# Setting PE's additional waits ahead of their group: the room that a place must leave, four times as large

## Chip, core and metric

The kernel runs on one core of one Trainium2 chip. The metric is the device time of one execution in microseconds (us), as the median of several runs; less is better. The core's engines are named as in the profile: PE (TensorE's matrix products), PEld (its weight loads), DVE (VectorE), ACT (ScalarE), POOL (GpSimd) and SP (SyncE, which issues DMAs here). Each engine works through its own queue of instructions in order, and the queues are kept together by semaphores: an instruction that finishes raises a counter, and another waits until the counter has reached a value.

## What is computed

Four residual steps on one sequence of 2048 positions with 512 features, bfloat16: attention, MLP, attention, MLP, with the same weights in both rounds.

```python
def _A_ref(x, wqkv, wo):
    B, S, D = x.shape
    H = 32; Dh = D // H; W = 256
    qkv = (lambda x, *d: x.transpose(*d))((x @ wqkv).reshape(B, S, 3, H, Dh), 2, 0, 3, 1, 4)
    q, k, v = qkv[0], qkv[1], qkv[2]
    scores = jnp.einsum("bhqd,bhkd->bhqk", q, k) * (Dh ** -0.5)
    idx = jnp.arange(S)
    mask = (idx[:, None] - idx[None, :] >= 0) & (idx[:, None] - idx[None, :] < W)
    scores = jnp.where(mask[None, None], scores, -1e9)
    p = _softmax(scores, axis=-1)
    o = jnp.einsum("bhqk,bhkd->bhqd", p, v)
    return (lambda x, *d: x.transpose(*d))(o, 0, 2, 1, 3).reshape(B, S, D) @ wo

def _B_ref(x, w1, b1, w2, b2):
    h = jnp.einsum("bsd,df->bsf", x, w1) + b1
    h = _gelu(h)
    return jnp.einsum("bsf,fd->bsd", h, w2) + b2

x = A_x
x = x + _A_ref(_layernorm(x, axis=-1), A_wqkv, A_wo)
x = x + _B_ref(_layernorm(x, axis=-1), B_w1, B_b1, B_w2, B_b2)
x = x + _A_ref(_layernorm(x, axis=-1), A_wqkv, A_wo)
x = x + _B_ref(_layernorm(x, axis=-1), B_w1, B_b1, B_w2, B_b2)
```

Each position attends to the 256 positions that end with itself, in 32 heads of 16 features. The MLP's inner width is 1792.

## The kernel before

**Tiles.** The sequence is cut into 16 tiles of 128 positions, which two rounds make 32 steps (`tau`), and into blocks `b` of two tiles. X stays in SBUF for the whole kernel. For each tile a layer norm is made on DVE and POOL (L740 to L750) and turned to put features on partitions: by PE against an identity (L768, `ident,xn` in the profile) or by a transpose on DVE and two DMAs (L757 to L764). PE then makes Q, K and V (`xnTA,Wqkv_sb`, `Wqkv_sb,xnTA` and `Wqkv_sb,xv`), which ACT and DVE take out of PSUM (L725, L727, L853). Attention makes scores in visits of 512 columns for four groups of heads (`QT,KT`, L952 to L959); each visit needs four PSUM banks, and two exponentials on ACT (L965) empty them into E. DVE or POOL mask E (L981). PE multiplies E with V (`E,Va`, L1000 to L1020), DVE turns and normalises the result (L1031 to L1041), PE projects it with Wo (`Wo_sb,OT`, L1069), and DVE adds it to X (L793). The MLP is two chains of products (`xnTB,W_sb`, L1098 and L1109, and `W_sb,gT`, L1121), with GELU on ACT and bias on DVE or ACT between them. The profile shows W1 and W2 both as W_sb, and nearly all products stand under line 32, where a helper records them.

**Order.** What runs where is written out by hand. `ORDER` (L425) is the sequence of some 3170 steps, `TURNS` (L594) says which of two engines takes a step that either could do, and `BANKS` (L610) gives the PSUM banks. `_List.run` (L233) goes through `ORDER` and books a start and an end for every step, from durations written beside the steps and a few constants. So the plan's times are a forecast in nanoseconds, computed when the program is made.

**Waits.** `_Sched.op` (L89) turns each step into a piece of its engine's program and works out which counters it must wait for. It sorts these waits by the planned end of the work that they wait on, latest first (L115), and drops each one that another already implies (L116). `self.when` holds the planned time at which a counter's value is visible (L120), and `start` the planned start of a step.

**Groups and slots.** One step of PE is a group of 1 to some 70 products, each a weight load and a product; a product's place in PE's program is called a slot in the code. `_Slots._next` (L25) puts the waits of a slot in front of its product. One wait can ride on the weight load itself; of several waits on one slot the others become instructions of their own in PE's queue, which the profile shows under line 27.

**Where PE's waits go.** `_Sched.spread` (L135) gives the first wait of a group, the latest by the plan, to the group's first product (L143 to L145). Each other wait is tried on slots ahead of the group, from the nearest back (L150), up to 96 of them (`LOOK`). The walk ends at a slot whose group starts, by the plan, too soon after the wait's work is visible, or whose group the wait's work itself depends on (L152). The first slot on the walk that holds no wait yet takes it (L154). If the walk ends without one, the wait stays on the group's own first product, together with the first. The room that a slot must leave is 1200 ns for a wait on a DMA and 150 ns for a wait on an engine.

Of the kernel before, what the change touches and what calls it, by code (L numbers as in the profile page):

```python
# [55 lines left out]
class _Sched:  # L56
# [78 lines left out]
    def spread(self):  # L135

        prog = self.prog["pe"]
        slots = [(k, i) for k, o in enumerate(prog) for i in range(o["n"])]
        first, taken = {}, {}
        for x, (k, i) in enumerate(slots):  # L140
            if i == 0:
                first[k] = x
        for k, o in enumerate(prog):  # L143
            if o["waits"]:
                taken[first[k]] = [o["waits"][0]]  # L145
        for k, o in enumerate(prog):
            for w in o["waits"][1:]:
                to = first[k]
                need = self.snap[w].get("pe", 0)
                for x in range(first[k] - 1, max(-1, first[k] - self.LOOK), -1):  # L150
                    k2, i2 = slots[x]
                    if need > k2 or self.when[w] + (1200.0 if w[0].startswith("dma") else 150.0) > prog[k2]["start"]:  # L152
                        break
                    if x not in taken:  # L154
                        to = x
                        break
                taken.setdefault(to, []).append(w)
        for o in prog:
            o["at"] = {}
        for x, ws in taken.items():  # L160
            k, i = slots[x]
            prog[k]["at"][i] = [(self.cnt_sem[c], v) for c, v in ws]
# [1046 lines left out]
```

## Time and profile before

| what | value |
|---|---|
| runs shown | 438.74, 438.5 and 439.74 us; median 438.74 |
| the profiled execution's own time | 439.42 us |
| its span, first to last instruction | 437.7 us |
| mean granted clock of TensorE | 0.996 |
| moved by DMA | 22.82 MB, mean 52 GB/s |

The profile is of one execution. A row of the groups names a line, an engine, an operation, what it writes and reads, and how often it ran; after the bar stand busy time, mean ns of one, and the idle time ahead of it with what ended it. A row of the timeline has start and duration in us, engine, line, operation and count, and in brackets the engine's idle time ahead of it with the work whose end released it; rows of one kind that follow each other are merged. A row of the waits names who waited for whom, with total us, number of times and the longest. PE's rows are the products with their pipeline, so a product of 0.38 us can have the next one 0.22 us behind it; PEld's rows are the loads, which overlap them; PEldq stands for instructions of the same queue that are neither.

### The profile page before, as it was taken

The numbers are of one execution on the slowest core, as the hardware profiler recorded it, in microseconds if no ns is written. First come the engines' busy times: TensorE is split into PE (matmuls) and PEld (weight loads), VectorE is DVE, ScalarE is ACT, GpSimd is POOL, SyncE is SP. The second block draws the span as 40 slices with busy tenths as digits, with TensorE's granted clock in tenths as the row PEclk, the third lists the DMA queues.
The fourth block names the chain that finished last, engine by engine and source line by source line (L and its number), as shares of the span: only waits on it lengthen the run. The fifth ranks groups of instructions, "written<-read, shape, count | busy, mean of one in ns | idle before, by whom it ended". The sixth has DMA issues, their size and how long they took to land.

```text
span 437.7 us, 18385 instructions
## 1 busy us (share of the span) xinstructions
PE 420.4 (96%) x8280; PEld 252.6 (58%) x8338; DVE 369.4 (84%) x752; ACT 391.7 (89%) x456; POOL 267.6 (61%) x293
## 2 busy tenths in 40 slices
PE   7999999999799999999999999999999999999996
PEld 5757757655554646555555555644566554454673
DVE  6999999999999998999899878898988883784722
ACT  3999999999999999899898999899889998999551
POOL 6788765958665847456489545774656397464030
PEclk9999999999899999999999999999999999999999
DMA  8930000001311031011031013001240003004001
GB/s 258 371 110 4 3 3 2 3 7 35 88 49 29 25 77 51 13 52 43 22 75 51 13 37 99 4 3 36 60 115 3 3 27 97 1 3 124 25 13 48
DMA packets 39899, 22.82 MB, mean 52 GB/s; under 512 B 24588, under 2 KB 39308, under 8 KB 39820
## 3 DMA queue, kind: packets, MB, share of 16 engines
q1 hardware_dynamic: 39404, 21.24, 16.6%
q8 instruction: 65, 1.06, 1.0%
q10 hardware_dynamic: 416, 0.39, 0.3%
q14 instruction: 14, 0.11, 0.1%
HBM read 13.77 MB, written 7.86 MB: 49 GB/s over the span
## 4 chain that ended last, share of the span: by engine, by line
PE 68%; ACT 24%; DVE 4%; issue 1%; DMA 1%; POOL 1%; ACTq 0%
PE ps L32 67%; ACT E L965 15%; ACT gT L1103 4%; ACT gT L1111 2%; ACT L1103 1%; ACT L965 1%; DMA X<-in_A_x_dram 1%; DVE E L981 1%; PE ps L36 1%; DVE stat L740 1%; DVE KT L853 1%; DVE TT L1031 1%; DVE X L793 0%; ACT L1111 0%; POOL E L981 0%
## 5 line engine op out<-in xcount | busy, mean ns | idle before, releaser
L965 ACT ACTIVATE E<-ps 128x1024 bf16<-128x1024 f32 x300 | 283.5, 1049 | 19.5 <-PE ps L32 18.6
L981 POOL TENSOR_TENSOR E<-E,mask 128x512 bf16<-128x512 bf16 (+1 forms) x132 | 142.1, 1091 | 72.5 <-DVE E L981 30.1
L32 PE MATMUL ps<-xnTB,W_sb 128*128 128x512 bf16 (+1 forms) x560 | 116.3, 337 | 0.2
L32 PE MATMUL ps<-W_sb,gT 128*128 128x512 bf16 (+2 forms) x418 | 106.4, 373 | 3.2 <-issue 2.5
L32 PE MATMUL ps<-xnTA,Wqkv_sb 128*128 128x256 bf16 (+1 forms) x544 | 74.5, 267 | 0.9 <-ACT E L965 0.5
L32 PEld LDWEIGHTS ps<-xnTB,W_sb 128*128 128x128 bf16 x560 | 51.7, 98 | 37.5 <-ACT E L965 0.7
L793 DVE TENSOR_TENSOR X<-X,ps 128x512 bf16<-128x512 bf16 x63 | 42.7, 679 | 27.2 <-PE ps L32 26.7
L32 PE MATMUL ps<-QT,KT 32*128 32x64 bf16 (+3 forms) x2392 | 60.7, 218 | 3.8 <-ACT E L965 2.7
L32 PEld LDWEIGHTS ps<-W_sb,gT 128*128 128x128 bf16 x462 | 40.8, 98 | 38.2 <-ACT E L965 0.5
L32 PEld LDWEIGHTS ps<-QT,KT 32*128 32x128 bf16 x2392 | 34.8, 93 | 47.6 <-ACT E L965 32.3
L981 DVE TENSOR_TENSOR E<-E,mask 128x512 bf16<-128x512 bf16 (+1 forms) x124 | 49.7, 422 | 11.3 <-ACT E L965 10.9
L32 PEld LDWEIGHTS ps<-xnTA,Wqkv_sb 128*128 128x128 bf16 x544 | 47.8, 98 | 16.5 <-ACT E L965 1.0
L1075 POOL TENSOR_TENSOR X<-X,b2b 128x512 bf16<-128x512 bf16 x32 | 36.8, 1154 | 27.6 <-DVE E L981 17.1
L744 POOL TENSOR_TENSOR statmv<-statmv,mhalf 128x1 f32<-128x1 f32 x64 | 35.8, 565 | 26.6 <-DVE statmv L742 26.6
L1100 DVE TENSOR_SCALAR gT<-ps,b1T 128x512 bf16<-128x512 f32 (+1 forms) x72 | 45.6, 650 | 3.9 <-PE ps L32 2.6
L32 PE MATMUL ps<-E,Va 64*17 64x64 bf16 (+3 forms) x3904 | 46.4, 230 | 1.9 <-ACT E L965 0.5
L1031 DVE STREAM_TRANSPOSE TT<-ps 128x1024 f32<-128x1024 f32 x32 | 39.8, 1244 | 8.7 <-PE ps L32 8.4
L1111 ACT ACTIVATE gT<-ps,b1T 128x512 bf16<-128x512 f32 (+1 forms) x68 | 36.5, 585 | 11.7 <-PE ps L32 11.6
L32 PEld LDWEIGHTS ps<-E,Va 64*17 64x17 bf16 x3904 | 37.1, 85 | 15.6 <-PE ps L32 3.9
L740 DVE BATCH_NORM_STATS2 stat<-X 128x6 f32<-128x512 bf16 x64 | 42.8, 675 | 2.6 <-DMA X<-in_A_x_dram 2.3
L853 DVE TENSOR_TENSOR KT<-ps,parmask 128x512 bf16<-128x512 f32 (+1 forms) x68 | 40.9, 644 | 2.6 <-PE ps L32 2.4
L1036 POOL TENSOR_TENSOR TM<-TT 128x512 bf16<-128x512 f32 x25 | 27.7, 1106 | 20.7 <-DVE TT L1034 11.2
(57 smaller groups left out, 383.4 us busy)
## 6 DMA issues: line engine op xcount, KB each, us to landing
scr_x<-xs_ SPq DMA_DIRECT2D x44, 128.0 KB, 1.7
W_sb<-in_B_w_dram SPq DMA_DIRECT2D x2, 1792.0 KB, 15.7
xnTB<-scr_x SPq DMA_DIRECT2D x26, 128.0 KB, 2.6
xnTA<-scr_x SPq DMA_DIRECT2D x18, 128.0 KB, 2.5
out_dram<-X SPq DMA_DIRECT2D x15, 128.0 KB, 1.9
Wqkv_sb<-in_A_wqkv_dram SPq DMA_DIRECT2D x4, 256.0 KB, 5.1
X<-in_A_x_dram SPq DMA_DIRECT2D x1, 1024.0 KB, 10.5
Wqkv_sb<-in_A_wqkv_dram SPq DMA_DIRECT2D x1, 512.0 KB, 6.6
```

What stands on the lines that cost most here:

```text
L32: return self.e.matmul(*a, **k)
L740: add("dve", lambda e, B: e.bn_stats(stat6[:, k6, 0:6], X[:, t, :]), 598, reads=["X%d" % t], writes=["st%d" % k6], prio=prio)
L744: add("pool", lambda e, B: e.tensor_tensor(out=statmv[:, m, 1:2], in0=statmv[:, m, 1:2], in1=mhalf[:], op=ALU.pow), 535, reads=["mv%d" % m ...
L793: add("dve", lambda e, B: e.tensor_tensor(out=X[:, t, :], in0=X[:, t, :], in1=ps[:, B[g][0], :], op=ALU.add), d_psum(512), reads=["X%d" % ...
L853: x = e.tensor_tensor(out=dst.rearrange("p (g s) (a k) -> p s g a k", s=2, a=2)[:, s], in0=src.rearrange("p (g s k) -> p s g k", s=2, k=HK ...
L965: add("act", lambda e, B, g_=g_, gi=gi: e.activation(E[:, 2 * gi : 2 * gi + 2, e0 : e0 + 512], ps[:, B[g_][0] : B[g_][0] + 2, :], AF.Exp, ...
L981: op = lambda e, B, Ew=Ew, Mw=Mw: e.tensor_tensor(out=Ew, in0=Ew, in1=Mw, op=ALU.mult)
L1031: add("dve", lambda e, B: e.transpose(TT[:, s].rearrange("p a c q d -> p a (c q d)"), ps[:, B[g][0] : B[g][0] + 2, :].rearrange("p a n -> ...
L1036: mul = lambda e, B: e.tensor_tensor(out=TM[:, sm].rearrange("p c q a d -> p a (c q) d"), in0=TT[:, s, :, :, :, 0:Dh].rearrange("p a c q d ...
L1075: add("pool", lambda e, B: e.tensor_tensor(out=X[:, t, :], in0=X[:, t, :], in1=b2b[:], op=ALU.add), 1110, reads=["X%d" % t, "b2b"], writes ...
L1100: add("dve", lambda e, B, g=g, fc=fc: e.tensor_scalar(out=gT[:, js % NG, fc, 0:M], in0=ps[:, B[g][0], 0:M], scalar1=b1T[:, fc : fc + 1], s ...
L1111: add("act", lambda e, B, g=g, fc=fc: e.activation(gT[:, js % NG, fc, 0:M], ps[:, B[g][0], 0:M], AF.Gelu_apprx_tanh, bias=b1T[:, fc : fc + ...
```

## The change

One number in `spread` is another: a slot ahead of a group takes a wait on an engine only if its group starts, by the plan, at least 600 ns after the waited-for work is visible, where it was 150 ns. The room for waits on DMAs stays 1200 ns. Waits that no longer find a slot stay on their group's own first product. The lists, the plan's times, the set of waits and everything on the other engines are as before.

```diff
@@ -149,7 +149,7 @@
                 need = self.snap[w].get("pe", 0)
                 for x in range(first[k] - 1, max(-1, first[k] - self.LOOK), -1):
                     k2, i2 = slots[x]
-                    if need > k2 or self.when[w] + (1200.0 if w[0].startswith("dma") else 150.0) > prog[k2]["start"]:
+                    if need > k2 or self.when[w] + (1200.0 if w[0].startswith("dma") else 600.0) > prog[k2]["start"]:
                         break
                     if x not in taken:
                         to = x
```

## The prediction

> **What bounds the kernel now.** I read the page's first and fourth parts, then the waits of PE over the whole span, then the same view from 120 us on.
>
> ```profile
> span 437.7 us, 18385 instructions
> PE 420.4 (96%) x8280; PEld 252.6 (58%) x8338; DVE 369.4 (84%) x752; ACT 391.7 (89%) x456; POOL 267.6 (61%) x293
> ...
> PE 68%; ACT 24%; DVE 4%; issue 1%; DMA 1%; POOL 1%; ACTq 0%
> ```
>
> PE is busy for 420.4 of 437.7 us and holds 68% of the chain that ended last. So PE sets the time, and a change of PE's waits can give back at most PE's idle time, 437.7 - 420.4 = 17.3 us, if it gives anything.
>
> ```profile
> PE ps L32 <- ACT E L965: 4.0, 8, 1.4
> PE ps L32 <- issue: 2.9, 18, 0.2
> ...
> PE ps L32 <- DVE X L793: 0.3, 1, 0.3
> PE ps L32 <- DVE KT L853: 0.2, 1, 0.2
> PE ps L32 <- DVE E L981: 0.2, 1, 0.2
> ```
> ```profile
> PE ps L32 <- issue: 2.7, 17, 0.2
> PE ps L32 <- DVE X L793: 0.3, 1, 0.3
> PE ps L32 <- PE ps L32: 0.3, 1, 0.3
> PE ps L32 <- DVE stat L740: 0.2, 1, 0.2
> ```
>
> The columns are total us, times, longest. The first fence is the whole span, the second 120 us to the end. The eight waits on the exponentials (4.0 us) all lie before 120 us. After it the matrix products were idle for another engine twice, 0.3 + 0.2 us, and once for PE's own earlier result, 0.3 us; the other 2.7 us have no releaser. So for three quarters of the kernel there is next to nothing that a better place of a wait could win.
>
> **What the change moves.** I worked the plan's own starts and ends out from the printed lists (the arithmetic of `_List.run`, `op` and `spread`). PE has 1627 groups with 8338 products, as many as the weight loads that the page counts for PEld. 486 groups wait, with 236 waits beyond their first. In the kernel before, 172 of the 236 sit on a product ahead of their group; 64 stay on their group's own first product, beside the first wait. A second wait on one product takes an instruction of its own, at L27:
>
> ```profile
> L27 PEldq EVENT_SEMAPHORE  x61: 51/51/51, 8.9 to 392.4; - x61
> ...
> L27 PEldq EVENT_SEMAPHORE  x37: 51/51/51, 120.0 to 392.4; - x37
> ```
>
> 61 such instructions (37 of them after 120 us) of 51 ns carry the 64 waits; a few carry two. [...]
>
> Of the 172 waits set back, 35 are on DMAs and keep their 1200 ns. Of the other 137, 71 have less than 600 ns of room on the product where they sit: 40 on DVE, 18 on ACT, 11 on POOL, 2 on PE. These 71 fall to their group's own first product. They belong to 71 different groups, none of which has a second wait there now, so each gets one L27 instruction: 61 + 71 = 132 in all. 34 go ahead of scores (QT,KT), 20 ahead of E,Va products, 17 ahead of projections, transposes and the like; 21 lie before 120 us, 50 after. Nothing else of the program changes: order, banks, engines and DMAs stay, and no other queue gets or loses an instruction.
>
> **Part removed: waiting too early.** A wait that sits ahead of its group can hold work that doesn't need it. By the times in the trace, 7 of the 71 were the last thing that the product in front waited for (at 60.7, 88.0, 202.7, 255.9, 326.4, 363.0 and 372.2 us). Two of them:
>
> ```profile
> 59.85 0.59 PEld L32 LDWEIGHTS ps<-W_sb,gT 128*128 128x128 bf16 x4
> 60.70 0.10 PEld L32 LDWEIGHTS ps<-W_sb,gT 128*128 128x128 bf16 x1 [0.26 <-DVE xnTB L725]
> 61.08 0.11 PEld L32 LDWEIGHTS ps<-QT,KT 32*128 32x128 bf16 x6 [0.28 <-ACT E L965]
> ```
> ```profile
> 59.91 1.24 PE L32 MATMUL ps<-W_sb,gT 128*128 128x512 bf16 x5
> ...
> 61.08 0.40 PE L32 MATMUL ps<-QT,KT 32*128 32x128 bf16 x16
> ```
> ```profile
> 202.29 0.21 PEld L32 LDWEIGHTS ps<-Wo_sb,OT 128*128 128x128 bf16 x2
> 202.68 0.10 PEld L32 LDWEIGHTS ps<-Wo_sb,OT 128*128 128x128 bf16 x1 [0.19 <-DVE X L793]
> 203.13 0.15 PEld L32 LDWEIGHTS ps<-QT,KT 32*128 32x128 bf16 x12 [0.35 <-ACT E L965]
> ```
>
> At 60.70 a product of W_sb and gT waits for a copy into xnTB that it doesn't read: that is the wait of the scores behind it. The last of the four loads before it starts at 59.85 + 0.59 - 0.10 = 60.34, so its load came 0.36 us later. But the scores' first load comes 61.08 - 60.34 = 0.74 us after that load, and the matmul row has no idle bracket (59.91 + 1.24 = 61.15, past 61.08). At 202.68 it is 203.13 - 202.40 = 0.73 us. Beside them a place where the set-back wait (on DVE) had long come, and one with an L27 instruction:
>
> ```profile
> 221.78 0.10 PEld L32 LDWEIGHTS ps<-W_sb,gT 128*128 128x128 bf16 x1
> 222.00 0.10 PEld L32 LDWEIGHTS ps<-Wo_sb,OT 128*128 128x128 bf16 x1
> 222.52 0.17 PEld L32 LDWEIGHTS ps<-QT,KT 32*128 32x128 bf16 x10 [0.42 <-ACT E L965]
> ```
> ```profile
> 259.66 0.75 PEld L32 LDWEIGHTS ps<-W_sb,gT 128*128 128x128 bf16 x4
> 260.83 0.12 PEld L32 LDWEIGHTS ps<-QT,KT 32*128 32x128 bf16 x8 [0.42 <-ACT E L965]
> ```
> ```profile
> L27 PEldq EVENT_SEMAPHORE  x1: 51/51/51, 260.6 to 260.6; - x1
> ```
>
> At 222 us no wait came late, and the same two steps are 222.52 - 221.78 = 0.74 us. So the late loads at 60.70 and 202.68 cost nothing: a load may come up to about 0.36 us after the one before it (the products themselves are 0.22 us apart) and the scores still start on time. It is the same at the other five, whose two steps also add up to 0.74 us. **Gain: 7 x 0 = 0 us.** When the loads come earlier, what is late next is what ends the 0.74 us now, the switch from full products to scores. From the other side, had every late load held the products, the gain would be the excess over 0.22 us, 0.14 us at 60.70 and 0.41 us for all seven.
>
> **Part added: 71 instructions of 51 ns.** At 260.6 us an L27 instruction stands between W_sb and QT,KT. The last of the four loads starts at 259.66 + 0.75 - 0.10 = 260.31, and the scores' first load 0.52 us behind it. Without one, at 222 us, it is 222.52 - 222.00 = 0.52 us. The 51 ns lie beside the running product. The cover is there in all 34 moves ahead of scores and in 19 of the 20 ahead of E,Va, since each stands at such a switch (the other one joins two E,Va groups and waits on PE itself); ahead of the other 17 the products in front, mostly 0.11 or 0.22 us apart, must cover it. The moved semaphore itself is there in time: in this trace all 71 came at least 0.29 us before their group's first load. Behind each new instruction the whole rest of PE's queue is held, and the exponentials on ACT wait for the scores:
>
> ```profile
> L965 ACT ACTIVATE E<-ps 128x1024 bf16<-128x1024 f32 x300 | 283.5, 1049 | 19.5 <-PE ps L32 18.6
> ```
>
> So if the cover is gone at a place, ACT gets its scores 51 ns later. There is one place in this trace where an L27 instruction lies in time that the products lost:
>
> ```profile
> L27 PEldq EVENT_SEMAPHORE  x1: 51/51/51, 109.8 to 109.8; - x1
> ...
> 109.88 0.40 PE L32 MATMUL ps<-QT,KT 32*128 32x64 bf16 x16 [0.27 <-ACT E L965]
> ```
>
> One of 61 pays, so 71 new ones pay 71 / 61 x 51 ns = 0.06 us. The ends are 0 and 71 x 51 ns = 3.6 us; I take 0.1 us, the value of the nearest rows, since the 37 of them after 120 us share 0.8 us of idle time that has a releaser at all.
>
> **Sum:** 0 gained, 0.1 us paid. The profiled execution took 439.42 us (span 437.7 and 1.7 us around it), so 439.5 for it; it is 0.7 us above the median of the runs shown. On the median, 438.74 + 0.1 = **438.8 us**.
>
> **Rivals.**
>
> *The new waits stand on PE's path* (slower). The place is the first product of the 71 groups, the price 51 ns each: 3.6 us for all, 442.4 us; half of them 1.8 us, 440.5 us. It decides where PE's queue has less than 51 ns of work in front when the instruction is reached, as at 109.8. For it: PE is 96% busy, and 17 of the moves have no switch to hide in. Against it: the equal 0.52 us, and 37 such instructions with nearly no idle time of the products. It must be over 1.3 us, more than a third of all places, to be seen. Chance 0.12.
>
> *Waiting later frees PE's clock* (faster). After idle stretches the granted clock fell:
>
> ```profile
> 115.29 0.40 PE L32 MATMUL ps<-QT,KT 32*128 32x128 bf16 x16 [1.37 <-ACT E L965]
> ```
> ```profile
> 116.90:120.30 3.40, 3.40 (x92) 2.22 (x74) 2.73 (x5) 3.03 (x4) 2.72 (x5) 0.50 0.25 82
> ```
>
> For 3.4 us PE had half its clock (the last columns: clock 0.50, DMA share, GB/s); what it lost is at most 1.7 us. If the idle time before were shorter or lay otherwise, it would go: 438.7 - 1.7 = 437.0 us. [...] Against it: the idle time there is ended by ACT, and the two moved waits in it (108.9 and 113.5 us) came over 0.8 us early. A second such stretch would be as much slower. Chance 0.08 for the loss going, 0.02 for one more.
>
> *PE's program is fetched at other points* (slower).
>
> ```profile
> q8 instruction: 65, 1.06, 1.0%
> ```
>
> 1.06 MB in 65 packets took 1.0% of 16 engines' 437.7 us, 1.08 us each. 71 more instructions move the points at which PE needs the next packet. No idle time of a packet's length is in the view of waits after 120 us, so fetches are covered now; one exposed would give 439.9, two 440.9 us. Chance 0.03 for two.
>
> *The change does nothing*: if L27 stays at x61, 438.7 us; that falls within the forecast.
>
> **How the numbers follow.** About 0.3%, 1.3 us, is what a measurement of this kernel can tell from no change. Within it: my forecast, 0.75. Slower by more: 0.12 + 0.02 + 0.03 = 0.17. Faster by more: 0.08. The range for 8 in 10 takes in the forecast with the spread of the runs shown (438.5 to 439.74), most of the gain of the clock, down to 437.4, and the events paying at a little over half the places, up to 440.8.
>
> **What would show it.** Right: L27 with x132; no bracket ended by DVE at the W_sb load near 60.7; 0.52 us from the last full load to the scores where the new instructions stand; the products' idle time within 1 us of 17.3. Wrong: idle brackets at first products of the 71 groups, or ACT's 18.6 us of waiting for PE grown by 1 us or more (the first rival); a clock row without the half (the second); idle time of about 1 us without a releaser (the third). A gain without any change of the clock would mean that early waits held PE by a way that the idle brackets don't show, and that my 0 was wrong.

## The result, and the profile after

The changed kernel takes **443.38 us** (median of 5 runs, 443.17 to 444.87), the kernel before 438.74 us (438.5 to 439.74): 4.64 us more, a ratio of 1.0108 with a 95% interval of 1.0094 to 1.0121. That is slower by over 0.3%, and outside the range of 437.4 to 440.8. The profiled execution of the changed kernel took 444.27 us with a span of 442.5 us, 4.8 us more than the span before.

The page's first rows, the instructions at L27 and PE's waits (total us, times, longest) over the whole span:

```profile
span 442.5 us, 18456 instructions
PE 423.0 (96%) x8280; PEld 253.4 (57%) x8338; DVE 370.3 (84%) x752; ACT 392.4 (89%) x456; POOL 267.8 (61%) x293
```
```profile
L27 PEldq EVENT_SEMAPHORE  x132: 51/51/51, 9.4 to 421.9; - x132
```
```profile
PE ps L32 <- issue: 5.1, 21, 1.3
PE ps L32 <- ACT E L965: 3.6, 7, 1.4
...
PE ps L32 <- DVE TT L1031: 0.8, 1, 0.8
```

The change did what it says: 61 + 71 = 132 instructions at L27. PE's idle time grew from 17.3 to 442.5 - 423.0 = 19.5 us, and the row that grew is the one without a releaser, from 2.9 us (longest 0.2) to 5.1 us (longest 1.3). The row `<- DVE TT L1031` (0.8 us) belongs to it: it is the stop at 314.1 us in the table below, where PEld's waits put the same 0.8 us down to issue. The other 2.6 us of the 4.8 stand as busy time on the page; the starts of the loads, further down, show them better. The longest of those 21 waits is here, in PE's products of the changed kernel; below it the same groups in the kernel before:

```profile
385.51 0.74 PE L32 MATMUL ps<-E,Va 64*17 64x64 bf16 x64
386.18 0.40 PE L32 MATMUL ps<-QT,KT 32*128 32x64 bf16 x16
386.51 0.72 PE L32 MATMUL ps<-E,Va 64*17 64x64 bf16 x59
388.55 0.21 PE L32 MATMUL ps<-E,Va 64*17 64x64 bf16 x5 [1.31 <-issue]
```
```profile
382.16 0.74 PE L32 MATMUL ps<-E,Va 64*17 64x64 bf16 x64
382.84 0.40 PE L32 MATMUL ps<-QT,KT 32*128 32x64 bf16 x16
383.17 0.74 PE L32 MATMUL ps<-E,Va 64*17 64x64 bf16 x64
383.84 1.04 PE L32 MATMUL ps<-xnTB,W_sb 128*128 128x512 bf16 x4
```

A group of 64 products stops after 59 of them. No wait stands there: the kernel puts none inside this group. So what was missing was not data but the next instructions.

Counting shows it. PE's program has two instructions for each of its 8338 products (the load and the product itself) and one for each at L27. I numbered them and looked where a load came later than the usual spacing with no wait in front that had just ended. In the changed kernel there are seven such places, and all have a number that leaves 191 to 193 when divided by 256:

| us | late by us | remainder | us since the end of the last packet on q8 |
|---|---|---|---|
| 101.7 | 0.42 | 192 | 1.46 |
| 113.2 | 1.01 | 191 | 1.41 |
| 263.2 | 0.12 | 192 | 1.30 |
| 286.2 | 0.42 | 193 | 1.68 |
| 314.1 | 0.83 | 191 | 1.41 |
| 326.1 | 0.14 | 193 | 1.53 |
| 388.5 | 1.54 | 191 | 1.47 |

They add up to 4.5 us. In the two rows with remainder 193 an instruction ahead of the load was held up first (a product at 285.93 us, with 0.26 us `<-issue`, and an L27 instruction at 325.9 us), 1.4 us after the packet. So at all seven PE went on 1.3 to 1.5 us after a packet had ended. q8 is a queue that brings instructions (`q8 instruction` on the page): 65 packets for PE's 16,808 instructions, one for every 258.6. With 16,977 of them (the late 240 below) and 17,040 (232 at the start) the pages count 66 packets, each time as many as there are numbers that leave 192. Two views of the stretch before the stop at 388.5 us, the windows and the DMA queues:

```profile
385.54:387.24 1.70, 1.70 (x140) 1.35 (x139) 1.34 (x2) 1.01 (x2) 1.70 (x3) 1.00 0.04 10
387.24:388.54 1.30, 0.00 (x0) 0.00 (x0) 0.00 (x0) 1.30 (x2) 1.30 (x2) 1.00 0.00 0
```
```profile
q8 instruction: 1, 0.02, 2.3%
```

Some 140 loads and as many products overlap these 1.7 us (second and third column); 128 of each, 256 instructions, lie between the two points. Then PE issued none for 1.3 us, and a single packet of instructions came within those 3.0 us. In the kernel before, the part that begins in the same groups takes 7.41 us, with two packets:

```profile
382.48:389.89 7.41, 7.36 (x155) 3.86 (x139) 5.41 (x10) 6.69 (x9) 5.65 (x6) 1.00 0.02 4
```
```profile
q8 instruction: 2, 0.03, 2.3%
```

So in these runs the program comes in parts of 256 instructions, by the remainders and by the count of packets. At each of the seven stops the last packet before it, which PE waited for, had begun only after PE crossed the point before (0.4 to 1.3 us after): no more than the next part was on its way. Where two points lie around E,Va products and scores, PE can run through a part in less time than the fetch needs: 1.7 us here, where 3.0 us passed from crossing one point to being able to cross the next. The 71 new instructions move the points along the program, by 1 after the first and by 71 after the last.

Two further items make up the 4.8 us. Some stops of the kernel before are gone, 0.15 to 0.19 us at 24, 98 and 286 us, and 0.58 us of the second stop is regained just behind it, where PE waited for ACT before. That leaves 4.5 - 0.5 - 0.6 = 3.4 us. And half clock lasted longer, 6.8 us where it was 3.4 us, with some 0.9 us lost between 114 and 119 us:

```profile
115.80:122.60 6.80, 5.98 (x193) 4.05 (x194) 5.04 (x9) 5.34 (x6) 5.21 (x7) 0.50 0.30 78
```

The remaining 0.5 us arises before 6 us, at the start-up products, ahead of the first L27 instruction (9.4 us), so it isn't the change's. With 3.4 + 0.9 + 0.5 = 4.8 us nothing is left over for the 51 ns of the new instructions.

### The profile page after: what moved, and what is told of

Its sections match the earlier page's. It is cut to its first block, busy times and chain, and to the rows that moved or that the text cites. A ratio compares the mean times of both kernels' runs of the same rounds, so it can differ in the third digit from the quotient of the medians.

```text
span 442.5 us, 18456 instructions
## 1 busy us (share of the span) xinstructions
PE 423.0 (96%) x8280; PEld 253.4 (57%) x8338; DVE 370.3 (84%) x752; ACT 392.4 (89%) x456; POOL 267.8 (61%) x293
## 4 chain that ended last, share of the span: by engine, by line
PE 63%; ACT 28%; DVE 4%; issue 2%; DMA 1%; POOL 1%; ACTq 0%
PE ps L32 62%; ACT E L965 17%; ACT gT L1103 5%; ACT gT L1111 3%; ACT L965 1%; ACT L1103 1%; DMA X<-in_A_x_dram 1%; DVE KT L853 1%; DVE TT L1031 1%; PE ps L36 1%; DVE E L981 1%; ACT L1111 1%; DVE stat L740 1%; DVE X L793 0%; POOL E L981 0%
## 5 line engine op out<-in xcount | busy, mean ns | idle before, releaser
L965 ACT ACTIVATE E<-ps 128x1024 bf16<-128x1024 f32 x300 | 283.9, 1040 | 22.3 <-PE ps L32 21.3
L32 PE MATMUL ps<-QT,KT 32*128 32x64 bf16 (+3 forms) x2392 | 61.6, 219 | 4.7 <-ACT E L965 2.7
L1031 DVE STREAM_TRANSPOSE TT<-ps 128x1024 f32<-128x1024 f32 x32 | 39.8, 1244 | 10.7 <-PE ps L32 10.4
```

Of the source, the lines that this page charges most:

```text
L32: return self.e.matmul(*a, **k)
L965: add("act", lambda e, B, g_=g_, gi=gi: e.activation(E[:, 2 * gi : 2 * gi + 2, e0 : e0 + 512], ps[:, B[g_][0] : B[g_][0] + 2, :], AF.Exp, ...
L1031: add("dve", lambda e, B: e.transpose(TT[:, s].rearrange("p a c q d -> p a (c q d)"), ps[:, B[g][0] : B[g][0] + 2, :].rearrange("p a n -> ...
```

## The experiments

Three theories: **fetch** (PE stops where it reaches a part of its program that has not come), **price** (each new instruction costs its 51 ns on PE's path), **place** (waits that come later in the order cost time themselves). What the fetch theory expects was worked out from the trace of before: the times of its loads, points every 256 instructions as counted above, and 3.45 us from crossing one to being able to cross the next. The 3.45 us are an estimate of the author's; at the seven stops above it was 3.0 to 4.0 us. Each median below stands beside the kernel before run on the same chip, with the ratio's 95% interval.

**Only the count, at the start.** All waits as before; 71 added instructions between the two start-up groups:

```diff
+        prog[1]["at"].setdefault(0, []).extend([(self.cnt_sem["dve"], 1)] * 143)
```

(L27 has x132 in this run, 61 + 71: one of the 143 waits needs no instruction, and two each share one.)

> The kernel before, all waits where they were, with 71 waits that are long satisfied put between PE's two start-up groups, so that all of PE's later program stands 71 instructions further on. Fetch theory (PE stops where its program crosses into a part of 256 instructions that has not been fetched, and 71 more instructions move these points into dense stretches): from the times of the groups in the trace of before, the points then fall where ten of them are reached too early, about 1 to 2 us each; 447 to 453 us. Price theory (each added instruction costs its 51 ns on PE's path): at the start PE waits for the first tiles anyway, so at most 71 x 51 ns = 3.6 us less that cover, 438.7 to 441. Place theory (waits that come later in the order cost time of their own): no wait was moved, 438.7.

Measured: 458.31 us against 438.58, ratio 1.0444 (1.0415 to 1.0474). So the fetch theory's 447 to 453 us is missed as well. In the profiled execution (457.88 us) PE's loads are 4.92 us later than in the kernel before from 14 us on, at the added instructions themselves, more than was expected, and 18.45 us later at the end. The 13.5 us between arise in a program in which every wait stands where it stood. PE's waits (the longest is the one at the start) and one of the stops:

```profile
PE ps L32 <- issue: 17.1, 29, 4.1
```
```profile
399.99 0.68 PE L32 MATMUL ps<-E,Va 64*17 64x128 bf16 x46
402.15 0.21 PE L32 MATMUL ps<-E,Va 64*17 64x64 bf16 x7 [1.49 <-issue]
```

Thirteen stops of 0.15 to 1.83 us sum to 15.2 us, all at remainders 191 to 193; some of it is regained behind them. The trace of before gave some 14 us for this shift. Price and place had at most 441 us, and nothing for the 13.5 us behind the start: both fail here.

**The same instructions, no wait moved.** Each of the 71 groups gets a satisfied wait instead:

```diff
+        for k, o in enumerate(prog):
+            for w in o["waits"][1:]:
+                for x in range(first[k] - 1, max(-1, first[k] - self.LOOK), -1):
+                    if w in taken.get(x, ()):
+                        if not w[0].startswith("dma") and self.when[w] + 600.0 > prog[slots[x][0]]["start"]:
+                            o["at"].setdefault(0, []).append((self.cnt_sem["dve"], 1))
+                        break
```

> The kernel before, with every wait where it was set back to, and a second, long satisfied wait on the first product of the same 71 groups. PE's program then has the same length and the same instructions at the same places as the changed kernel's, but no wait is moved. Fetch theory: as the changed kernel, 442.5 to 444. Price theory: also as the changed kernel. Place theory: as before, 438.7, since only satisfied waits were added.

Measured: 443.55 us against 438.58, ratio 1.0091 (1.0062 to 1.0119), the changed kernel's median within 0.2 us. The interval, 2.7 to 5.2 us, is wide because one of the four runs, the only one at full clock, took 441.51 us; the other three took 443.48 to 443.63 us at 0.995 or 0.996. The long stop is at the same product:

```profile
385.56 0.72 PE L32 MATMUL ps<-E,Va 64*17 64x64 bf16 x59
387.90 0.21 PE L32 MATMUL ps<-E,Va 64*17 64x64 bf16 x5 [1.61 <-issue]
```

So 71 more instructions at these places give the loss with no wait moved, and moving the 71 waits adds or wins nothing that these runs can tell. The place theory falls.

**The change on a part of the groups.** Once on the groups before 120 us alone, once on the others:

```diff
-(1200.0 if w[0].startswith("dma") else 150.0)
+(1200.0 if w[0].startswith("dma") else 600.0 if k < 418 else 150.0)
```

and with `k >= 418`.

> The change on the groups before 120 us alone: 21 waits fall to their own group. Fetch theory: of the stops of the changed kernel only those near 101 and 112 us come, about 0.4 and 1.0 us, with the slower clock after them; the later points move by 21 only and stay covered: 439.8 to 441. Price theory: 21 x 51 ns = 1.1 us spread over 21 places, 439.8. Place theory: under half of the loss, about 21 / 71 of it, 440.1. The trace tells them apart: two long stops inside groups, or 21 small ones.

> The change on the groups after 120 us alone: 50 waits fall to their own group. Fetch theory: the stops near 101 and 112 us are gone, and as the count starts at 0 at 120 us the later points move by 0 to 50 instead of 21 to 71; by the times of before only the one near 385 us is left, about 0.7 us: 438.7 to 440. Price theory: 50 x 51 ns = 2.6 us, 441.3. Place theory: 50 / 71 of the loss, 442.

Measured: 440.65 us, ratio 1.0033 (1.0018 to 1.0048), for the 21 waits, and 439.75 us, ratio 1.0029 (1.0016 to 1.0043), for the 50, both against 438.58. With 21 waits the stops at 101.8 and 113.4 us are there (0.88 and 1.00 us; the second below), and a third of 0.46 us at 323.7 us that the working had not shown. With 50 they are not; there is 0.84 us at 386.6 us, as expected, and again 0.53 us at 323.7. Both times are in the fetch theory's ranges; price and place had 441.3 and 442 us for the 50.

```profile
112.33 0.37 PE L32 MATMUL ps<-QT,KT 32*128 32x64 bf16 x11 [0.67 <-ACT E L965]
113.39 0.31 PE L32 MATMUL ps<-QT,KT 32*128 32x256 bf16 x5 [0.69 <-issue]
```
```profile
111.94 0.40 PE L32 MATMUL ps<-QT,KT 32*128 32x64 bf16 x16 [0.67 <-ACT E L965]
112.86 1.05 PE L32 MATMUL ps<-xnTA,Wqkv_sb 128*128 128x256 bf16 x8 [0.51 <-ACT E L965]
```

The first fence has the 21 waits, the second the 50: the same scores, with and without a stop inside the group. The 50 cost no more than the 21, which no equal price for each instruction gives, and by the medians both together cost less than the whole change (2.07 + 1.17 = 3.24 of 4.64 us).

**The 51 ns by themselves.** From 395 us on only three fetch points are left. Every one of PE's last 240 groups gets an instruction of its own:

```diff
+        for o in prog[1387:]:
+            at = o["at"].setdefault(0, [])
+            at.extend([(self.cnt_sem["dve"], 1)] * (1 if at else 2))
```

> The kernel before, and a long satisfied wait as an instruction of its own ahead of each of the last 240 groups of PE (from 395 us on). Price theory: 240 x 51 ns = 12 us, or what part of it stands on the path: 444 to 451. Fetch theory: there are three fetch points left in this stretch, and by the times of before all three have room for the shift: 438.7 to 439.7, that is, the 51 ns lie beside the running products.

Measured: 439.32 us against 438.66, ratio 1.0010 (0.9995 to 1.0025). L27 over the whole span:

```profile
L27 PEldq EVENT_SEMAPHORE  x301: 51/51/51, 8.8 to 432.1; - x151
```

240 x 51 ns = 12.2 us are added to PE's queue, and 0.7 us or nothing to the time: at most 1.1 us by the interval's upper end, 5 ns each. Most of these groups (224 of 240) are MLP products, so this holds for them first of all. For the scores the changed kernel itself has the row to see: at 262.7 us an L27 instruction stands ahead of scores, and their load comes 262.94 - (261.54 + 0.98 - 0.10) = 0.52 us after the last full one, as without.

```profile
261.54 0.98 PEld L32 LDWEIGHTS ps<-W_sb,gT 128*128 128x128 bf16 x6
262.94 0.34 PEld L32 LDWEIGHTS ps<-QT,KT 32*128 32x128 bf16 x16 [0.42 <-ACT E L965]
```

**Points turned by a whole part, and back by 24.** Does any shift cost, or only one that puts points at bad places? 256 added instructions at the start leave the points where they were; the changed kernel with 232 of them has its points 24 instructions earlier.

```diff
+        prog[1]["at"].setdefault(0, []).extend([(self.cnt_sem["dve"], 1)] * 513)
```

(465 waits for the changed kernel's 232.)

> The kernel before with 256 long satisfied waits between PE's start-up groups. The fetch points are 256 instructions apart, so the later program stands as it did before against them. 71 such waits delayed the start by 4.9 us in the run above, of which 71 x 51 ns = 3.6 us were the waits; 256 x 51 ns = 13.1 us and 1.3 us give 14.4 us. Fetch theory: 438.7 + 14.4 = 453, less than the 458.3 us of 71 waits at the same place. If shifting by any amount cost time, it would be 458 + 9.4 = 468.

> The changed kernel with 232 long satisfied waits at the same place, so that its fetch points stand 24 instructions earlier in its program than they do in the changed kernel (232 is 256 less 24). To be compared with the kernel before with 256 such waits, from which it differs by 24 x 51 ns = 1.2 us less at the start. Fetch theory: by the times of before the stops then sum to 1.4 us, against 0.8 us for the kernel before: 0.6 us more of stops and 1.2 us less at the start, 0.6 us faster than the other one, within 1.5 us. Price theory: 3.6 - 1.2 = 2.4 us slower than the other. Place theory: 4.6 - 1.2 = 3.4 us slower.

Measured: 464.39 us (ratio 1.0584, 1.0564 to 1.0605) and 464.38 us (1.0585, 1.0565 to 1.0606). The start took far longer than expected, and with it the expected 453 us is missed: an added instruction here cost some 0.1 us (the starts of two L27 instructions in a row lie 0.11 us apart, though each shows 51 ns), and PE's wait at the start is 24.3 and 21.7 us.

```profile
PE ps L32 <- issue: 24.3, 1, 24.3
PE ps L32 <- ACT E L966: 3.7, 7, 1.4
```
```profile
PE ps L32 <- issue: 22.6, 3, 21.7
PE ps L32 <- ACT E L966: 3.7, 7, 1.4
```

What is to be compared lies behind the start. In the first kernel the loads are 25.1 us later than in the kernel before from 14 us of its time on, and 24.8 us at the end: a shift by 256 costs nothing, where one by 71 cost 13.5 us. In the second they are 23.6 us later and 25.2 us at the end: of the 4.8 us that the changed kernel's profiled execution lost, 1.6 us are left with all 71 waits moved. The equal medians don't decide by themselves, since the start differs by 2.6 us and not by the 1.2 us that was reckoned with. Behind the start the second kernel loses 1.6 + 0.3 = 1.9 us more than the first, where fetch had 0.6, price 3.6 and place 4.6 us: nearest to fetch, but three times its figure. Its stops, the longest 0.99 us, again stand at remainders 191 to 193.

**A shift meant to help.** 8 instructions, at a place where PE waits for its tile:

```diff
+        prog[3]["at"].setdefault(0, []).extend([(self.cnt_sem["dve"], 1)] * 16)
```

> The kernel before with 8 long satisfied waits ahead of PE's second transpose group, in the 1 us in which PE waits for its tile anyway, so that all later fetch points move by 8 instructions. Fetch theory: the small stops of before near 24, 98 and 286 us (0.15 to 0.19 us each) come or go, by the times of before the shift leaves 0.2 us of stops where there are 0.5 to 0.8: 438.0 to 438.7. Price theory: 438.7, as PE waits there. Not one of the theories has it over 439.2.

Measured: 439.65 us against 438.66, ratio 1.0017 (1.0004 to 1.0030): a miss, all theories had less. In its profiled execution the three stops of before are gone, two of 0.12 and 0.13 us have come, and the span is 437.5 us, 0.2 us less. But eight of its 12 runs have a mean clock of 0.996 (439.27 to 440.72 us), against four of the 23 of the kernel before; the other four are its quickest, 438.50 to 439.10 us. The profiled execution of the kernel before, which has 3.4 us at half clock, shows 0.996 too. So by the mean clocks such a stretch came more often here, and that was more than the stops were worth; why it came more often was not found. No version here beats the kernel before.

## Why the prediction was wrong

**What the change moves** was right: 132 instructions, in 71 groups.

**The part removed** was right at 0 us. In the changed kernel the load at 60.7 us is no longer late, and the scores behind it come as they did, with no gain:

```profile
60.23 0.80 PEld L32 LDWEIGHTS ps<-W_sb,gT 128*128 128x128 bf16 x5
61.46 0.26 PEld L32 LDWEIGHTS ps<-QT,KT 32*128 32x128 bf16 x16 [0.42 <-ACT E L965]
```

**The part added** was right in what it looked at, 0.1 us for 71 x 51 ns; the late 240 bound it at 5 ns each. It wasn't all that an added instruction does.

**The step that failed is the third rival**, "PE's program is fetched at other points", with a chance of 0.03 for the 2.2 us of two exposed fetches; the sum held nothing for it. Measured, its stops are 3.4 of the 4.8 us between the two profiled executions. It named the mechanism and mis-sized it three times over. First, the price was the packet, 1.08 us; what PE waits for is the time from crossing one point to being able to cross the next, which at the seven stops above was 3.0 to 4.0 us: mostly 0.9 to 1.3 us until the packet starts, 0.9 to 1.8 us for it and 1.3 to 1.5 us behind its end. Second, "no idle time of a packet's length is in the view of waits after 120 us, so fetches are covered now" takes idle time for room. A fetch that is just in time shows no idle time: at 162.4 us the kernel before crossed a point 1.56 us after its packet's end and 3.85 us after the point before, with no load late. And PE does 256 instructions of E,Va products and scores in 1.7 us. The kernel before had its points at places where this was just enough; the waits there couldn't show by how little. Third, the points don't move one by one: every added instruction moves all that follow, and seven places lost time, 4.5 us in all, instead of two. The prediction's own sign for this rival, idle time of about 1 us without a releaser, is what came (1.3 us).

The plan that the prediction worked out holds this mechanism. In `_List.run` (L277 to L286) PE's instructions are counted at 2.0115 for each product, a point stands after 194 of them and after every 256 more, and PE waits at a point until a part is loaded, 3550 ns after the point before (`CODE`, L194; 6200 ns up to 23 us). These are the plan's figures; measured were remainders of 191 to 193, 3.0 to 4.0 us at the seven stops, and 6.5 us from the first point to the second and from there to the third in the kernel before (11.1, 17.6 and 24.1 us). So the plan reckons with the points, and as printed it has 0.01 us of such stops in all. The 2.0115 stays when 71 instructions are added, so the plan doesn't notice them. As an estimate with the plan's arithmetic, but with two instructions for each product and one for each wait beyond a product's first, the stops sum to 1.4 us for the kernel before and to 5.2 us for the changed one (at 99, 110, 281, 309, 321 and 383 us of the plan, six of the seven stops above), and the changed plan ends 3.6 us later.

What could have shown it in the trace of before: the three late loads at 24.1, 97.9 and 285.5 us, of 0.15 to 0.19 us and without a wait, whose places in the program leave 192 when divided by 256. They were below what the waits of PE list, and I had not counted places.

**The first rival** (51 ns on the path) came close to the measured time, 442.4 against 443.4 us, by accident: the late 240 and the equal 0.52 us speak against it. **The second** (the clock) was given 0.08 for the stretch at half clock going and 0.02 for one more; it was the latter that came: half clock lasted twice as long and is some 0.9 us of the loss in the profiled execution. That the idle time ahead of it decides on half clock, as this rival has it, no run shows. Between runs of one kernel it weighs as much: of the ten runs with the 50 waits, six at a clock of 1.000 took 439.40 to 439.80 us and four at 0.995 or 0.996 took 440.67 to 441.14 us. With the same count and no wait moved, the one run at full clock took 2.0 us less than the other three. All five runs of the changed kernel have 0.988 to 0.995, so the clock has a part in its median too, and how large a part is not known. Whether the stop at 113 us brings this on was not separated: with the 21 waits the stop is there and four of ten runs keep the full clock, and with the 8 added instructions it is not and most lose it. That part of the cause stays open.

## What to carry to other kernels

An instruction added to PE's long unrolled queue had two costs here: its own 51 ns, of which at most 5 ns showed in the late 240, and the shift of everything behind it against the points where the program is fetched (71 at the start cost 13.5 us behind them, 256 none). Before a change of some 50 instructions, count where those points fall and compare the time that the engine takes for the instructions between two of them with the fetch's. Here 256 instructions of E,Va products and scores took 1.7 us and the fetch 3.0 us, and that was too little. Where a plan of the kernel counts instructions by an average, put the new count in first. When such a change makes a kernel slower, run the same number of instructions without the change's meaning: here that gave the whole loss at once, 443.55 us against 443.38.

## What the runs showed that was not expected

- Where PE stopped for its program in the changed kernel, 3.0 to 4.0 us lay between one fetch point and the next, and PE went on 1.3 to 1.5 us after the end of the packet. 71 instructions at the start cost 13.5 us behind it, 256 none.
- 240 instructions of 51 ns in PE's queue cost 5 ns each or less.
- At the start, where PE had nothing else to do, instructions of this kind that carry two waits took some 0.1 us each: 256 of them instead of 232 delayed the start by 24.9 instead of 22.3 us.
